# A two-layer recurrent kernel: 64x128 tiles for the first part of its one-layer score blocks, filler matmuls in the first two steps and the last, and its own order for the first and last steps

## The chip, the cores and the metric

The kernel runs on one core of a Trainium2 chip. The metric is the device time of one execution in microseconds (us). TensorE (PE in the profile) multiplies matrices into PSUM, which has eight banks here; ScalarE (ACT) and VectorE (DVE) copy results out of PSUM and do the softmax and layer norms; GpSimd (POOL) does small copies; SyncE (SP) issues nearly all transfers. An engine runs its own queue in order and waits on semaphores for the others.

## The reference, cut to what matters

```python
def _A_ref(x, mem0, Wq, Wk, Wv, Wo, seg_len):      # 64 segments of 32 rows, 16 heads of 256
    mem = mem0                                      # 8 rows
    for s in range(n_seg):
        xs = x[:, s * seg_len:(s + 1) * seg_len, :]
        h = jnp.concatenate([mem, xs], axis=1)      # 40 rows of 448
        q, k, v = (einsum('btd,dhe->bhte', h, W) for W in (Wq, Wk, Wv))
        scores = einsum('bhqe,bhke->bhqk', q, k) * scale    # masked: memory seen by all, rest causal
        p = _softmax(scores)
        o = einsum('bhte,hed->btd', einsum('bhqk,bhke->bhqe', p, v), Wo)
        mem = o[:, :M, :]                           # carried to the next segment
        outs.append(o[:, M:, :])

def _B_ref(x, W_gate, W_up, W_down):                # 448 -> 1792 -> 448
    gate, up = x @ W_gate, x @ W_up
    return (relu(gate) * up) @ W_down

x = x + _A_ref(_layernorm(x), ...);  x = x + _B_ref(_layernorm(x), ...)
x = x + _A_ref(_layernorm(x), ...);  x = x + _B_ref(_layernorm(x), ...)   # the same weights again
```

The loops above are shortened; x has 2048 rows. The memory carried from segment to segment makes each A layer a chain of 64 steps.

## The kernel before, in words

The two A layers run interleaved. Step t works on segment t of layer 0 and segment t - 4 of layer 1 (`LAG`, line 29), so there are 68 steps. Steps 0 to 3 have layer 0 alone and steps 64 to 67 layer 1 alone: the eight one-layer steps, in which the moving operand of most matmuls has 40 columns (the 40 rows of one segment) and not 80.

In `setup` (line 602) the weights come in by SP and are multiplied once: Wq with Wk into M, 56 blocks of 128 columns (`Mw`, and for the last 64 of the 448 rows `M3`), and Wv with Wo into N (`Nw`). N's products are still being made while step 0 goes on. Then a step does this:

- `t_block` (line 905) makes T = M times h, 48 + 8 blocks in three groups (`BLOCKS`, line 967). In the first two groups the rows 384 to 447 come first: `first` (line 920) multiplies them as 64x64 tiles, four matmuls for a pair of blocks, in four quarters of the array. `rest` (line 935) adds the other three 128-row parts at 128x128. `t_copies` (line 949) brings the result to `TTm` and `TTs`.
- `s_mem` (line 979) makes the scores of the 8 memory rows and their softmax, `p_t_mem` (line 1050) transposes the probabilities on TensorE, `u_mem` (line 1067) multiplies them with h, and `un_mem` (line 1080) with N in 56 matmuls of 128x32 tiles. `hi` and `lo` are its result as two bf16 parts. From these `m_t` (line 1099) and `m_nat` (line 1120) make the memory rows for the next step. This is the chain from step to step.
- `s_seg` (line 1001), `seg_pt` (line 1040) and `u_seg` (line 1152) do the same for the 32 rows of the segment; the transpose is a transfer (`tdma`, line 900), in the last step four TensorE transposes.
- After each odd step, `un` (line 1195) multiplies the segments' rows with N, `halves` (line 1188) adds the two halves of its PSUM bank and x on DVE, `ln_b` (line 878) normalizes, and `b_layer` (line 1233) does B, its last part named b_down. The last step has two of these b_layers.

`warm` (line 894) issues n matmuls of the identity with 512 columns, whose result nobody reads. It is used once, in `un` of the last pair: `S.warm(8, O.res(), [])`, after the call of `halves`. The matmuls name `un`'s bank O as read, which orders them behind `un`.

What stands where is decided when the program is built. Each operation is recorded with what it reads and writes, with a cost and a tile mode (`mm`, line 806); `_Order.run` (line 323) then lists all of them, each time taking among the operations that could start first the one with the smallest key. It picks PSUM banks, and ACT or DVE where both may copy. The key of a TensorE operation is a number by hand, `SLOT` (line 177), by name and by step modulo 4, plus a period of 86000 for each four steps; other keys are worked out from those that follow. `BIAS` (line 163) adds a number by kind of operation; TensorE operations of the steps before 4 and from 64 on have biases of their own (`@a`, `@z`; `bias_keys`, line 218). Changing these numbers changes no operation, only its place.

`_Sched._need` (line 68) then makes the semaphore waits in that order. It has one rule for PSUM that matters here:

```python
if r[0] == "ps":
    for src, val in self.readers.get(r, {}).items():
        if src != eng:
            want(src, val)
```

An operation that reads a bank also waits for those reads of another engine that stand before it in the order.

Of the kernel before, what the change touches and what calls it, by code (L numbers as in the profile page):

```python
# [44 lines left out]
class _Sched:  # L45
# [118 lines left out]
    "t_block@a": 1812, "t_blockm+": -9357, "t_blocks+": -8, "s_mem+": -142986, "p_t_mem@a": 31328, "p_t_mem+": -7192,  # L164
    "u_mem@a": 13521, "u_mem+": 747, "un_mem@a": -12628, "un_mem+": -15687, "un_memh+": -12449, "m_t@a": 6986,
    "m_t+": 6465, "m_tk+": -7932, "s_seg@a": 8100, "s_seg+": -15857, "seg_pt+": -131, "u_seg@a": 3317,
    "u_seg0+": -34358, "u_seg1+": -19122, "u_seg2+": 20412, "u_seg3+": 10778, "m_nat@a": 16787, "m_nat+": 67952,
    "t_block0f+": 11522, "t_block0r+": -14766, "t_block1r+": 16356, "ln_a+": 2229, "ln_ac+": -36153, "un@a": 57889,
    "un+": -5801, "ln_b+": -22707, "b_layer@a": -6365, "b_layer+": 479, "b_down@a": -28772, "b_down+": -16128,
    "m_natx+": 65420, "m_nat@z": -27634, "s_mem@z": 9161, "p_t_mem@z": -19432, "u_mem@z": -334, "un_mem@z": 8381,  # L170
    "m_t@z": 18252, "s_seg@z": -4933, "u_seg@z": 6743, "un@z": -14160, "b_layer@z": 39068, "b_down@z": -1631,
    "seg_pt@z": -26944, "ln_b@z": 196, "stay": 33066, "win": 142,
# [5 lines left out]
    "t_block0f.0@0": 23150, "t_block0r.0@0": 20466, "t_block0r.1@0": 10373, "t_block0r.2@0": -118963,  # L178
    "t_block0r.3@0": -102813, "t_block0r.4@0": -15176, "t_block0r.5@0": 95232, "t_block1f.0@0": 88326,
    "t_block1r.0@0": 70572, "t_block1r.1@0": -90708, "t_block1r.2@0": -669, "t_block1r.3@0": 23477,  # L180
    "t_block2r.0@0": 105637, "s_mem.0@0": -153732, "p_t_mem.0@0": -26811, "u_mem.0@0": -7044, "un_mem.0@0": 68017,
    "m_t.0@0": -385871, "s_seg.0@0": 180805, "u_seg0.0@0": 16616, "u_seg1.0@0": -3087, "u_seg2.0@0": 182854,
    "u_seg3.0@0": -7016, "m_nat.0@1": 15351, "t_block0f.0@1": -101435, "t_block0r.0@1": 175650,
    "t_block0r.1@1": -16550, "t_block0r.2@1": -78417, "t_block0r.3@1": -96693, "t_block0r.4@1": -96697,
    "t_block0r.5@1": -76748, "t_block1f.0@1": 94756, "t_block1r.0@1": -93576, "t_block1r.1@1": -61388,
    "t_block1r.2@1": 13060, "t_block1r.3@1": 192482, "t_block2r.0@1": 98249, "s_mem.0@1": 6005,
    "p_t_mem.0@1": -100695, "u_mem.0@1": 172343, "un_mem.0@1": 413220, "m_t.0@1": 76060, "s_seg.0@1": 89640,
    "u_seg0.0@1": 96587, "u_seg1.0@1": -148969, "u_seg2.0@1": 71131, "u_seg3.0@1": -99947, "un0.0@1": 269897,
    "un0.1@1": -174852, "un0.2@1": 156565, "un0.3@1": -89383, "un1.0@1": 70834, "un1.1@1": 69072, "un1.2@1": -29917,
    "un1.3@1": 26881, "un2.0@1": -89787, "un2.1@1": -86447, "un2.2@1": -10845, "un2.3@1": 13517, "un3.0@1": 89653,  # L190
    "un3.1@1": 89684, "b_layerf.0@1": 94811, "b_layer.0@1": 48867, "b_layer.1@1": 96741, "b_layerf.1@1": 109098,
    "b_layer.2@1": -3240, "b_layer.3@1": 70642, "b_down.0@1": 354372, "b_down.1@1": 72900, "b_down.2@1": 254015,
    "b_down.3@1": 240246, "b_down.4@1": 326259, "b_down.5@1": 354136, "b_down.6@1": 78849, "m_nat.0@2": 168132,
    "t_block0f.0@2": -10118, "t_block0r.0@2": -98052, "t_block0r.1@2": -41109, "t_block0r.2@2": 66134,
    "t_block0r.3@2": 13073, "t_block0r.4@2": -14618, "t_block0r.5@2": -188807, "t_block1f.0@2": -3221,
    "t_block1r.0@2": -1996, "t_block1r.1@2": -186700, "t_block1r.2@2": 70640, "t_block1r.3@2": -74211,
    "t_block2r.0@2": 16205, "s_mem.0@2": -92464, "p_t_mem.0@2": -20075, "u_mem.0@2": -252353, "un_mem.0@2": -101434,
    "m_t.0@2": 84256, "s_seg.0@2": 96377, "u_seg0.0@2": 90135, "u_seg1.0@2": 97804, "u_seg2.0@2": 182858,
    "u_seg3.0@2": 260389, "m_nat.0@3": 151329, "t_block0f.0@3": -2977, "t_block0r.0@3": -188538,
    "t_block0r.1@3": 75914, "t_block0r.2@3": -96292, "t_block0r.3@3": 6194, "t_block0r.4@3": -75085,  # L200
    "t_block0r.5@3": 69297, "t_block1f.0@3": -185930, "t_block1r.0@3": 111423, "t_block1r.1@3": -36939,
    "t_block1r.2@3": 10926, "t_block1r.3@3": 370, "t_block2r.0@3": 12228, "s_mem.0@3": -124071, "p_t_mem.0@3": 180760,
    "u_mem.0@3": 6506, "un_mem.0@3": 65274, "m_t.0@3": -389, "s_seg.0@3": -12148, "u_seg0.0@3": -75151,
    "u_seg1.0@3": 176089, "u_seg2.0@3": 78879, "u_seg3.0@3": 340369, "un0.0@3": -161383, "un0.1@3": -95386,
    "un0.2@3": 323286, "un0.3@3": 5996, "un1.0@3": 11452, "un1.1@3": 76963, "un1.2@3": -93171, "un1.3@3": -179086,
    "un2.0@3": 162572, "un2.1@3": -2533, "un2.2@3": -15402, "un2.3@3": 334269, "un3.0@3": -77062, "un3.1@3": 94056,
    "b_layerf.0@3": 350365, "b_layer.0@3": 277881, "b_layer.1@3": 268897, "b_layerf.1@3": 354905,
    "b_layer.2@3": 181729, "b_layer.3@3": 192495, "b_down.0@3": 101118, "b_down.1@3": 346959, "b_down.2@3": -2948,
    "b_down.3@3": -287771, "b_down.4@3": 93426, "b_down.5@3": 159732, "b_down.6@3": 83157, "m_nat.0@0": -484,
    "un0.4@3": -268098, "un0.5@3": -13365, "un0.6@3": 248971, "un0.7@3": -102719, "un1.4@3": 260089, "un1.5@3": -4388,  # L210
    "un1.6@3": -67736, "un1.7@3": -9258, "un2.4@3": 265064, "un2.5@3": 334268, "un2.6@3": 332162, "un2.7@3": 163179,
    "un3.2@3": 8603, "un3.3@3": -7565, "b_layer.4@3": -10753, "b_layer.5@3": 79668, "b_layer.6@3": 131945,
    "b_layer.7@3": 253283, "b_layer.4@1": 182601, "b_layer.5@1": 61111, "b_layer.6@1": 10905, "b_layer.7@1": -174890,
    "seg_pt.0@3": -162209, "un.0@3": 195399, "ln_b.0@1": 303926,
# [3 lines left out]
def bias_keys(o):  # L218
    if not o.cat:
        return []  # L220
    if o.kind != "pe":
        return [o.cat + o.sub + "+"]
    return [o.cat + "@a"] if o.t < LAG else [o.cat + "@z"] if o.t >= NSEG else []
# [19 lines left out]
class _Order:  # L243
# [13 lines left out]
    def add(self, kind, eng, cost, fn, rd, wr, name=None, mode=0, lat=None, alt=None, base=(0, 0)):  # L257
        o = _Op()
        o.kind, o.eng, o.cost, o.fn, o.rd, o.wr, o.name, o.mode = kind, eng, cost, fn, list(rd), list(wr), name, mode
        o.alt, o.base = alt, base  # L260
        o.succs, o.np, o.alloc, o.fixed, o.lat, o.cat, o.sub, o.t = [], 0, [], None, lat, self.cat, self.sub, self.t
        o.slot = None
        if kind == "pe" and o.cat:
            name = o.cat + o.sub
            i = self.count[name] = self.count.get(name, -1) + 1
            o.slot = f"{name}.{i}@{o.t % 4}"
        self.ops.append(o)
        return o
# [195 lines left out]
def MM(out, lhsT, rhs, **kw):  # L464
    return (out, lhsT, rhs, kw)


class _Kernel:
# [16 lines left out]
    def alloc(self):  # L485
# [37 lines left out]
        self.lo = self.sb("lo", [128, D])  # L523
        self.ident = self.sb("ident", [128, 128])
# [369 lines left out]
    def warm(self, n, rd, wr):  # L894

        S = self
        T = S.tile("R", 1)
        S.mm(lambda: [MM(T.b()[:, 0:512], S.ident[:, :], S.N[:, 0:2, 0:256], start=True, stop=True) for _ in range(n)], n * S.pitch(512), rd, T.res() + wr)
# [6 lines left out]
    def t_block(self, t, units):  # L905
# [14 lines left out]
        def first():  # L920
            out = []
            for a, b in zip(range(0, len(units), 2), range(1, len(units), 2)):
                for j in range(units[a][2]):
                    for o, x in ((0, a), (0, b), (1, a), (1, b)):
                        c, u0, m = units[x]
                        side, slot = S.PLACE[16 * c + u0 + j]
                        h, g = slice(64 * side, 64 * side + 64), slice(64 * o, 64 * o + 64)
# [3 lines left out]
        if pair:  # L931
            S.mm(first, sum(u[2] for u in units[::2]) * S.pitch(n) + 25.0, rd, [r for x in R for r in x.res()] + [k for u in units for k in keys(*u)], mode=3)
# [46 lines left out]
    def s_mem(self, t):  # L979
# [7 lines left out]
             [("TTm",) + k for k in S.TKEYS] + [("hTx", pp, s, l) for l in range(l0, l1)] + S.mkeys(pp, s, l0, l1), C.res())  # L987
# [13 lines left out]
    def s_seg(self, t):  # L1001
# [5 lines left out]
        def mms():  # L1007
            b = G.b()
            out = []
            for l in range(l0, l1):  # L1010
# [9 lines left out]
             [("mask", 0), ("TTsz", 0), ("TTsz", 1)] + S.mkeys(pp, s, l0, l1), G.res())  # L1020
# [19 lines left out]
    def seg_pt(self, t):  # L1040
        S = self
        if t == NSTEP - 1:

            T = S.pe_transpose([("Ps",)], lambda a: S.Ps[:, a, :], [("PTs",)])
# [5 lines left out]
    def p_t_mem(self, t):  # L1050
# [3 lines left out]
        S.mm(lambda: [MM(pT()[:, 0:128], S.Pm[:, :], S.ident[:, :], is_transpose=True)], 60.0, [("Pm",), ("ident",)], C.res() + [("PTm",)])  # L1054
# [12 lines left out]
    def u_mem(self, t):  # L1067
# [6 lines left out]
             [r for l in C for r in C[l].res()] + [("UTm", S.win(t), l) for l in C], mode=3)  # L1074
# [291 lines left out]
```

## Time and profile before

| what | value |
|---|---|
| median of three runs | 1564.83 us (1560.64 to 1566.0) |
| profiled execution, its own time | 1565.71 us |
| its span | 1563.9 us |
| PE busy | 1505.9 us, 96% of the span, 37969 matmuls |
| weight loads (PEld) busy | 1106.3 us, 71% |
| DVE and ACT busy | 868.0 us (56%) and 858.3 us (55%) |
| chain that ended last | 92% PE, 3% DVE, 2% SP's queue, 2% ACT |
| mean granted TensorE clock | 0.99 |

The profile is one execution. Its page gives busy time and granted clock in slices, and the costliest groups of instructions; the trace behind it gives each instruction's start and what it waited for. All matmuls stand under line 138, as one helper issues them, so they are told apart by tile names: b is a PSUM bank, `big` holds the B weights, the segments' U and, early, some of the attention weights. "Nw,UTm" are `un_mem`, "Nw,big" `un` (early also N's products), "hT,Mw" and "hT,M" the T blocks, "xBT,big" and "big,hB" b_layer.

### The profile page before, as it was taken

The numbers are of one execution on the slowest core, as the hardware profiler recorded it, in microseconds if no ns is written. First come the engines' busy times: TensorE is split into PE (matmuls) and PEld (weight loads), VectorE is DVE, ScalarE is ACT, GpSimd is POOL, SyncE is SP. The second block draws the span as 40 slices with busy tenths as digits, with TensorE's granted clock in tenths as the row PEclk, the third lists the DMA queues.
The fourth block names the chain that finished last, engine by engine and source line by source line (L and its number), as shares of the span: only waits on it lengthen the run. The fifth ranks groups of instructions, "written<-read, shape, count | busy, mean of one in ns | idle before, by whom it ended". The sixth has DMA issues, their size and how long they took to land.

```text
span 1563.9 us, 81992 instructions
## 1 busy us (share of the span) xinstructions
PE 1505.9 (96%) x37969; PEld 1106.3 (71%) x37969; DVE 868.0 (56%) x2353; ACT 858.3 (55%) x2599; POOL 112.0 (7%) x259
## 2 busy tenths in 40 slices
PE   5889999999999999999999999999999999999997
PEld 2457667777677777777677777777677777777665
DVE  7434565655555655555555655555564655555554
ACT  5734555655555565655555565555555555555432
POOL 4000000000000000000000000000000000000000
PEclk9989999999999999999999999999999999999998
DMA  8841001000010100000011100101010100000000
GB/s 182 205 117 35 19 18 20 18 17 16 20 20 12 25 15 20 17 15 20 16 20 15 24 15 16 19 16 21 16 21 14 22 18 15 15 18 19 15 19 14
DMA packets 129735, 46.01 MB, mean 29 GB/s; under 512 B 117736, under 2 KB 129264, under 8 KB 129392
## 3 DMA queue, kind: packets, MB, share of 16 engines
q1 hardware_dynamic: 129040, 40.53, 12.4%
q8 instruction: 298, 4.88, 1.3%
q14 instruction: 45, 0.37, 0.1%
q10 hardware_dynamic: 352, 0.24, 0.1%
HBM read 10.33 MB, written 1.84 MB: 8 GB/s over the span
## 4 chain that ended last, share of the span: by engine, by line
PE 92%; DVE 3%; SPq 2%; ACT 2%; issue 1%; DMA 1%; POOL 0%; POOLq 0%; DVEq 0%
PE b L138 92%; SPq L622 2%; ACT hi L1096 1%; ACT big L798 1%; DVE UTm L799 1%; DMA Nw<-in_A_Wo_dram 0%; DVE selm L658 0%; DMA PTs<-Ps 0%; DVE seln L661 0%; DVE stat L845 0%; DVE part L1192 0%; DVE lo L1097 0%; ACT UTm L798 0%; DVE big L799 0%; DVE xn L852 0%
## 5 line engine op out<-in xcount | busy, mean ns | idle before, releaser
L138 PE MATMUL b<-hT,Mw 128*128 128x80 bf16 (+1 forms) x11424 | 436.7, 200 | 9.2 <-issue 8.6
L138 PEld LDWEIGHTS b<-hT,Mw 128*128 128x128 bf16 x11424 | 415.3, 100 | 22.7 <-issue 14.3
L138 PE MATMUL b<-Nw,big 128*32 128x448 bf16 (+1 forms) x3540 | 295.1, 356 | 1.8 <-DVE big L799 0.8
L798 ACT ACTIVATE TTs<-b 128x320 bf16<-128x320 f32 (+5 forms) x658 | 278.4, 426 | 3.7 <-PE b L138 3.7
L798 ACT ACTIVATE TTm<-b 128x80 bf16<-128x80 f32 (+5 forms) x658 | 153.2, 235 | 137.7 <-PE b L138 131.9
L138 PEld LDWEIGHTS b<-Nw,big 128*32 128x32 bf16 (+1 forms) x3540 | 136.4, 97 | 108.8 <-issue 2.4
L138 PE MATMUL b<-xBT,big 128*128 128x128 bf16 (+3 forms) x4900 | 208.7, 215 | 0.7 <-ACT xBT L798 0.7
L138 PEld LDWEIGHTS b<-xBT,big 128*128 128x128 bf16 (+1 forms) x4900 | 187.6, 102 | 19.3 <-issue 7.1
L138 PE MATMUL b<-Nw,UTm 128*32 128x448 bf16 x3752 | 193.5, 358 | 5.3 <-DVE UTm L799 3.6
L138 PEld LDWEIGHTS b<-Nw,UTm 128*32 128x32 bf16 x3752 | 97.2, 98 | 91.2 <-DVE UTm L799 10.0
L798 ACT ACTIVATE big<-b 128x512 bf16<-128x512 f32 (+1 forms) x258 | 128.5, 560 | 35.2 <-PE b L138 35.0
L799 DVE CAST TTm<-b 64x64 bf16<-64x64 f32 (+4 forms) x226 | 48.6, 216 | 176.3 <-PE b L138 174.7
L138 PE MATMUL b<-hT,M 64*64 64x80 bf16 (+2 forms) x7208 | 142.8, 198 | 2.0 <-DVE M L799 1.2
L138 PEld LDWEIGHTS b<-hT,M 64*64 64x64 bf16 (+1 forms) x7208 | 110.9, 108 | 28.0 <-ACT hT L798 7.1
L799 POOL COPY hK<-xn 32x448 bf16<-32x448 bf16 x136 | 75.1, 552 | 657.3 <-DVE xn L852 651.0
L798 ACT ACTIVATE UTm<-b 128x512 bf16<-128x512 f32 (+1 forms) x144 | 78.3, 567 | 74.3 <-PE b L138 74.3
L1263 ACT ACTIVATE gT<-b 128x512 bf16<-128x512 f32 (+2 forms) x128 | 69.4, 542 | 62.1 <-PE b L138 50.2
L138 PE MATMUL b<-big,hB 128*128 128x448 bf16 (+1 forms) x574 | 100.1, 354 | 0.7 <-DVE hB L1264 0.7
L1264 DVE TENSOR_TENSOR hB<-gT,b 128x512 bf16<-128x512 bf16 (+2 forms) x128 | 79.3, 619 | 38.1 <-ACT gT L1263 21.8
L798 ACT ACTIVATE hT<-b 64x16 bf16<-64x16 f32 (+1 forms) x134 | 24.0, 179 | 125.9 <-DVE hT L799 88.0
L799 DVE CAST TTs<-b 64x256 bf16<-64x256 f32 (+4 forms) x226 | 90.5, 401 | 2.7 <-PE b L138 2.6
L1096 ACT ACTIVATE hi<-b 128x448 bf16<-128x448 f32 x67 | 36.5, 544 | 91.6 <-PE b L138 91.6
(112 smaller groups left out, 1625.4 us busy)
## 6 DMA issues: line engine op xcount, KB each, us to landing
big<-in_A_Wo_dram SPq DMA_DIRECT2D x3, 896.0 KB, 6.0
out_dram<-ys SPq DMA_DIRECT2D x32, 56.0 KB, 2.0
big<-in_B_W_up_dram SPq DMA_DIRECT2D x7, 224.0 KB, 2.9
big<-in_B_W_gate_dram SPq DMA_DIRECT2D x7, 224.0 KB, 3.3
big<-in_B_W_down_dram SPq DMA_DIRECT2D x7, 224.0 KB, 2.6
XA<-in_A_x_dram SPq DMA_DIRECT2D x28, 56.0 KB, 2.3
PTs<-Ps SPq DMA_TRANSPOSE x67, 2.4
Nw<-in_A_Wo_dram SPq DMA_DIRECT2D x1, 896.0 KB, 6.1
```

The costliest lines, as they stand in the source:

```text
L138: ins = E.matmul(out, lhsT=lhsT, rhs=rhs, **kw)
L622: S.q.add("dma", ("sp",), {"sp": 6200.0 if w == "Wv" and q else 4100.0}, lambda E: E.dma_start_transpose(out=st[w, q], in_=src[w][:, q * 1 ...
L798: return E.activation(out(), src(), ACT.Copy)
L799: return E.tensor_copy(out(), src())
L1096: S.act(lambda E: E.activation(S.hi[:, :], C.b()[:, 0:D], ACT.Copy), D, C.res(), [("hi",)])
L1263: S.act(lambda E, g=g, R=R, n=n: E.activation(S.gT[:, g, 0:n], R[0].b()[:, 0:n], ACT.Relu), n, R[0].res(), [("gT", g)])
L1264: S.dve(lambda E, g=g, R=R, n=n, fcs=fcs: E.tensor_tensor(S.hB[:, fcs[0]:fcs[-1] + 1, 0:w], S.gT[:, g, 0:n].rearrange("p (a b) -> p a b", ...
```

## The change

Five things:

- In one-layer steps `first` uses tiles of 64 rows by 128 columns: two matmuls for a pair of blocks in place of four. Two-layer steps keep 64x64.
- `fill` puts `warm(2)` calls, each an operation of its own with a slot, into steps 0 and 1 (two behind `s_mem`, one behind `u_mem`) and into step 67 (three behind `s_seg`). `p_t_mem`, `un_mem` and the last `seg_pt` name ("filled", t) as read, so that the fillers come before them on TensorE. `warm` multiplies M in place of N.
- The slots of steps 0 to 3 and 64 to 67 are named apart (`@a0`, `@z3`), and all slots have new numbers: 491 in place of 175. The biases of TensorE operations are gone; the others have new numbers.
- `hi` and `lo` can be one stacked part (`stacked`), which is switched off: it returns False.
- Two SBUF tiles for that, `sumA` and `sumB`, unused.

```diff
 def bias_keys(o):
     if not o.cat:
         return []
-    if o.kind != "pe":
-        return [o.cat + o.sub + "+"]
-    return [o.cat + "@a"] if o.t < LAG else [o.cat + "@z"] if o.t >= NSEG else []
+    return [] if o.kind == "pe" else [o.cat + o.sub + "+"]
...
-            o.slot = f"{name}.{i}@{o.t % 4}"
+            o.slot = f"{name}.{i}@" + (f"a{o.t}" if o.t < LAG else f"z{o.t - NSEG}" if o.t >= NSEG else str(o.t % 4))
...
-        S.mm(lambda: [MM(T.b()[:, 0:512], S.ident[:, :], S.N[:, 0:2, 0:256], start=True, stop=True) for _ in range(n)], n * S.pitch(512), rd, T.res() + wr)
+        S.mm(lambda: [MM(T.b()[:, 0:512], S.ident[:, :], S.M[:, 0, 0:4, :], start=True, stop=True) for _ in range(n)], n * S.pitch(512), rd, T.res() + wr)
+
+    def fill(self, t, n):
+        S = self
+        if t < 2 or t == NSTEP - 1:
+            cat, S.q.cat = S.q.cat, "fill" + S.q.cat
+            for _ in range(n):
+                S.warm(2, [("gap", t)], [("filled", t)])
+            S.q.cat = cat
...
-                    for o, x in ((0, a), (0, b), (1, a), (1, b)):
+                    for o, x in ((0, a), (0, b), (1, a), (1, b)) if l1 - l0 == 2 else ((-1, a), (-1, b)):
                         c, u0, m = units[x]
                         side, slot = S.PLACE[16 * c + u0 + j]
-                        h, g = slice(64 * side, 64 * side + 64), slice(64 * o, 64 * o + 64)
+                        h, g = slice(64 * side, 64 * side + 64), slice(64 * o, 64 * o + 64) if o >= 0 else slice(0, 128)
...
-             [("TTm",) + k for k in S.TKEYS] + ... + S.mkeys(pp, s, l0, l1), C.res())
+             [("TTm",) + k for k in S.TKEYS] + ... + S.mkeys(pp, s, l0, l1), C.res() + [("gap", t)])
+        S.fill(t, 2)
...
+        if t == NSTEP - 1:
+            S.fill(t, 3)
...
-            T = S.pe_transpose([("Ps",)], lambda a: S.Ps[:, a, :], [("PTs",)])
+            T = S.pe_transpose([("Ps",), ("filled", t)], lambda a: S.Ps[:, a, :], [("PTs",)])
...
-        S.mm(lambda: [MM(pT()[:, 0:128], S.Pm[:, :], S.ident[:, :], is_transpose=True)], 60.0, [("Pm",), ("ident",)], C.res() + [("PTm",)])
+        S.mm(lambda: [MM(pT()[:, 0:128], S.Pm[:, :], S.ident[:, :], is_transpose=True)], 60.0, [("Pm",), ("ident",), ("filled", t)], C.res() + [("PTm",)])
```

The order that is built from it, against the order before: TensorE has 37569 matmuls in place of 37969, SP's queue is the same but for one exchanged pair near the end. In the first steps the last N products stand behind `s_mem` of step 0, not ahead of it. In the middle the operations are the same, with some of `un`'s matmuls a few places away. At the end `un`'s last 112 matmuls stand together, 48 b_layer matmuls follow, then the eight of `warm`, and 20 b_down matmuls stand between the last transposes and the last b_layer.

## The prediction

> **What bounds the kernel now.** I read first the page's strip of 40 slices, for where TensorE is idle or slow.
>
> ```profile
> PE   5889999999999999999999999999999999999997
> ...
> PEclk9989999999999999999999999999999999999998
> ```
>
> Only the first three slices and the last are below nine tenths; the granted clock dips there too. Next the busy time by stage (length of the stretch, then busy time and instructions of PE, weight loads, DVE, ACT, POOL, then clock, DMA share, GB/s).
>
> ```profile
> 78.40:96.00 17.60, 13.22 (x377) 9.13 (x377) 7.04 (x29) 5.45 (x21) 0.18 (x1) 0.86 0.32 89
> 96.00:115.00 19.00, 15.95 (x409) 10.23 (x413) 7.02 (x29) 5.97 (x23) 0.18 (x1) 0.77 0.51 151
> ...
> 223.90:311.80 87.90, 87.30 (x2224) 65.62 (x2224) 49.79 (x131) 50.27 (x152) 5.77 (x15) 1.00 0.10 18
> ...
> 1536.00:1564.00 28.00, 22.82 (x471) 13.63 (x468) 8.69 (x16) 5.06 (x10) 0.00 (x0) 0.80 0.03 6
> ```
>
> A period of four steps in the middle takes 88 us, with PE busy for 87.3 at full clock: only its own work counts there. At the ends PE idles and the clock falls to 0.77. So I read the TensorE timeline of the first steps (start, duration, tile shape, count; in brackets the idle time before and what ended it).
>
> ```profile
> 81.87 4.06 PE L138 MATMUL b<-Nw,UTm 128*32 128x448 bf16 x56 [0.64 <-ACT UTm L798]
> 88.33 0.66 PE L138 MATMUL b<-hT,M 64*64 64x40 bf16 x60 [0.33 <-ACT hT L798]
> 88.92 2.19 PE L138 MATMUL b<-hT,Mw 128*128 128x40 bf16 x81
> 93.88 2.03 PE L138 MATMUL b<-hT,Mw 128*128 128x40 bf16 x63 [1.49 <-issue]
> 98.20 0.29 PE L138 MATMUL b<-ident,Pm 128*128 128x128 bf16 x1 [1.08 <-DVE Pm L999]
> 100.02 5.21 PE L138 MATMUL b<-Nw,UTm 128*32 128x448 bf16 x56 [0.64 <-ACT UTm L798]
> 118.23 2.82 PE L138 MATMUL b<-Nw,UTm 128*32 128x448 bf16 x56
> ```
>
> The same 56 matmuls take 2.82 us at full clock, 4.06 in step 0 and 5.21 in step 1. The trace's clock record drops to one half at 81.0 (3.4 us), 94.65 (10.2 us), 132.2 (3.4 us) and 1535.1 (10.2 us), each time behind idle time. The 1.49 us before 93.88 is a wait for nothing shown ("issue"); seven such, of 6.05 us together, lie in one-layer steps (1.49, 0.36, 0.46, 1.38, 0.70, 0.82, 0.84). Last the end, on PE and DVE:
>
> ```profile
> 1533.42 0.51 PE L138 MATMUL b<-PTs,hK 40*64 40x512 bf16 x4
> 1535.66 0.61 PE L138 MATMUL b<-ident,Ps 128*128 128x128 bf16 x4 [1.73 <-DVE Ps L1038]
> ...
> 1541.19 5.22 PE L138 MATMUL b<-Nw,big 128*32 128x448 bf16 x64
> 1546.24 0.36 PE L138 MATMUL b<-big,hB 128*32 128x448 bf16 x4
> 1546.43 2.44 PE L138 MATMUL b<-Nw,big 128*32 128x448 bf16 x48
> 1548.80 1.90 PE L138 MATMUL b<-Nw,ident 128*128 128x512 bf16 x8
> ...
> 1550.74 0.62 DVE L1192 TENSOR_TENSOR part<-b,XA 64x448 f32<-64x448 f32 x1 [8.12 <-PE b L138]
> ```
>
> 1.73 us idle, then ten at half clock (64 matmuls in 5.05 us, 48 in 2.37). And DVE starts on `un`'s result only at 1550.74, though its last matmul ended near 1548.9: in this order the eight `warm` matmuls stand in front, name that bank as read, and DVE's semaphore value is theirs.
>
> **What the skill says.** "TensorE: Matmul & The Clock Gate", Part 1: the clock falls to one half after an idle window of about 3.4 us and rises after a busy one. The trace agrees on 0.5 and on 3.4 us steps; it also drops after windows with only 1.0 to 1.7 us of idle time. Its section on Weight-path perf modes has fast weight load on when there are 128 weight columns, and "TensorEngine Tiling (Array Packing)", Restrictions, has column tiling switch it off. That fits 64x64 at 40 columns: (0.59 us less 0.09 for a switch) / 60 = 8.3 ns each, 33 ns a group of four, against 2.04 / 81 = 25 ns for a full 128x128 matmul. The same page, Key Properties: a change of mode drains the array; start to start, 64x64 to 128x128 takes 115 ns, some 90 too many.
>
> **The change, part by part**, against the profiled execution's 1565.71 us (span 1563.9), 0.9 above the median.
>
> *64-row, 128-column tiles.* In the 8 one-layer steps 100 matmuls of 64x64 become 50 of 64 rows by 128 columns: 800 become 400, in 200 pairs. The trace has no such pair. Bounds: 25.5 ns with fast load (200 x -7.5 = -1.5 us); 66 ns if a tile takes 128 columns at the 33 ns per 64 seen (+6.6). I take -1.3.
>
> *Fewer instructions.* T blocks of one layer go from 316 to 266 matmuls. The trace's instruction queue brings 16 KB, 128 matmuls with their loads, every 3.4 to 4 us at its fastest: 27 ns a matmul, 8.5 us for 316, used in about 6.7. For 266 it is 7.2 against 6.5. The shortfall falls from 1.8 to 0.7 us a step, so I take 60% of the 6.05 us away: -3.6 (ends 0 and -6).
>
> *Fillers, steps 0 and 1.* Each `warm(2)` is two 512-column matmuls; from the eight above, 1.72 / 8 = 0.215 us each. In step 1 four (0.86) stand in the 1.08 us softmax gap and two (0.43, plus switches) in the 0.64 us before `un_mem`: 0 at full clock; at half clock the four would take 1.72 and cost 0.6. In step 0 the new order puts thirteen N products behind `s_mem`, so the gaps of 0.30, 1.08 and 0.32 are filled with due work (-1.70) and four fillers are pure cost (+0.86): -0.84. Behind them on ACT stand eleven copies of 0.49 us and PTm, UTm; banks are what could run late.
>
> *Clock.* With step 0 busy, `un_mem` takes 2.82: -1.24. Step 1's drop cost 2.39 in `un_mem` and some 0.7 around; it followed the 1.49 us stall; half taken, -1.5. Step 3's (140 matmuls in 4.56 us, 56 x 8.8 + 84 x 29.3 ns, start to start at full clock, = 2.96) followed the 1.38 us stall; half, -0.8.
>
> *End.* Six fillers (1.29), four u_seg and 24 b_layer matmuls now stand between `s_seg` and the transposes: the 1.73 us gap is closed, -0.44. The half clock then has no cause. What stood in it: `un` 2.2 us too long, b_layer 0.98 + 0.69, u_seg 0.7, transposes 0.3: -4.8. In the new order 48 b_layer matmuls precede the eight `warm`; DVE waits for `un` alone: -1.76, less 0.4, as 20 b_down matmuls now stand before the last b_layer: -1.4.
>
> *Mode switches.* 796 become 783: -1.2.
>
> *Tables.* In the middle the new order has the same matmuls in the same tiles with the same switches, 2224 a period; `un` matmuls move by a few places beside m_t and T blocks, and remain at least 1.9 us where the uncovered hi/lo wait at 163.5 was 1.30. ACT and DVE exchange one or two copies of a period, at 50 of 88 us busy; POOL takes one copy earlier; SP's order is unchanged but for one pair at the end. 0, with 15 periods x 0.2 = 3 us either way.
>
> Sum: 1.3 + 3.6 + 0.84 + 1.24 + 1.5 + 0.8 + 0.44 + 4.8 + 1.4 + 1.2 = 17.1 us. I give back 2.5 for waits that the new order makes itself (bank waits in step 0, m_nat among the T blocks of step 66): 1565.7 - 14.6 = **1551 us**, 0.9% under the median.
>
> **Rivals.**
> *The clock still falls at the end.* The windows run free of the program, and a 40-row u_seg or a stall may count as idle. For: it fell at 132.2 after 0.9 us of idle time in the window. Against: with the gap closed only two issue stalls are left between 1523 and the end of `un`. 4.8 and about 1 more stay: 1557.
> *The head doesn't gain.* Issue stalls come with the place of a refill and not with the rate, and step 1's clock with them: 3.6 + 1.5 + 0.8 + 1.24 stay: 1558. With both, 1564: no change. For: a 1.06 us stall at 1314 in a two-layer step. Against: seven of them in eight short steps.
> *Slower: the new tiles load slowly.* The clock page's LDWEIGHTS section prices a load at columns / 1.2 ns, 107 ns for 128; if both of a pair are paid in turn, 200 x (214 - 33) = +36 us, 1589. It decides above about 33 + 13300 / 200 = 100 ns a pair. Against: 64x64 loads of 64 columns overlap fourfold (33 ns for four), and full 128-column loads keep a 25 ns pace.
>
> **Chances and range.** Forecast 0.60 (own range 1546 to 1555); clock falls at the end 0.15; no gain in the head 0.08; both 0.07; slow loads or a middle slower by over 1 us a period 0.07; better than forecast 0.03. Faster by over 0.3% (under 1560.1; a run of this kernel can't tell less, its three lie 5.4 us apart): 0.83; within 0.3%: 0.10; slower: 0.07. 1545 to 1561 holds 8 in 10.
>
> **What would show it.** 64x128 pairs near 25 ns; `un_mem` of steps 0 and 1 at 2.8 us; issue stalls of the one-layer steps under 3 us in all; no clock drop from 1530 to 1550; DVE's last part<-b,XA within 0.3 us of `un`'s end; middle periods of 88.3 us in the mean, as before. Wrong if they exceed 88.6, if pairs take over 40 ns, or if step 0's `un_mem` waits for Nw copies beyond 82.

## The result, and the profile after

The kernel after takes 1539.99 us (median of four runs, 1539.38 to 1542.49), the kernel before beside it 1562.74: the ratio is 0.9858, with a 95% interval of 0.983 to 0.9887. That is 22.7 us less, where 13.8 less than the median shown were forecast, and the time lies under the lower end of the range, 1545. The sign was right, and the mechanism in the main; the size was too small. Measured again later, the kernel after took 1542.99 us, ratio 0.9876 (0.9853 to 0.9899), 19.8 less.

The profiled execution after took 1539.38 us, with a span of 1537.6. The strip of its page, in 40 slices:

```profile
PE   5999999999999999999999999999999999999998
...
PEclk9999999999999999999999999999999999999999
```

Only the first slice and the last are now below nine tenths. The clock reads nine tenths or more in every slice, and the record behind the strip is full from 36.3 us to 1538.2. This is one execution, with a mean clock of 0.999; the other runs of this kernel here and below read 0.997 to 0.999, so by estimate most of them have one or two stretches of 3.4 us at half clock more, at places not known. The busy time by stage, with the columns as before (length, then busy time and instructions of PE, weight loads, DVE, ACT, POOL, then clock, DMA share and GB/s); the stretches are step 1's and step 2's chain, one period of four steps, and the last 28 us:

```profile
75.00:89.60 14.60, 13.44 (x340) 8.95 (x337) 7.04 (x26) 7.02 (x23) 0.18 (x1) 1.00 0.38 106
89.60:105.70 16.10, 14.85 (x376) 9.93 (x381) 7.28 (x34) 5.79 (x21) 0.18 (x1) 1.00 0.57 159
212.97:300.77 87.80, 86.89 (x2220) 65.54 (x2224) 49.80 (x130) 49.31 (x150) 5.28 (x14) 1.00 0.08 18
1509.60:1537.60 28.00, 23.99 (x640) 16.13 (x637) 12.88 (x31) 10.24 (x32) 0.00 (x0) 1.00 0.08 14
```

The clock reads 1.00 where before it read 0.86, 0.77 and 0.80, and the last 28 us hold 640 matmuls where they held 471. The TensorE timeline of the first steps (start, duration, tile shape, count, idle time before and what ended it):

```profile
78.53 2.83 PE L138 MATMUL b<-Nw,UTm 128*32 128x448 bf16 x56
...
90.55 0.81 PE L138 MATMUL b<-Mw,ident 128*128 128x512 bf16 x3
91.57 0.23 PE L138 MATMUL b<-ident,Pm 128*128 128x128 bf16 x1 [0.21 <-DVE Pm L1077]
...
93.14 2.83 PE L138 MATMUL b<-Nw,UTm 128*32 128x448 bf16 x56
...
99.20 0.54 PE L138 MATMUL b<-hT,M 64*128 64x40 bf16 x30
99.67 1.70 PE L138 MATMUL b<-hT,Mw 128*128 128x40 bf16 x60
```

`un_mem` takes 2.83 us in both steps (4.06 and 5.21 before). The fillers ("Mw,ident", four in the program; a few matmuls have no record) leave 0.21 us of the 1.08 us before the transpose of Pm. The 30 matmuls of 64x128 take 0.47 us from start to start, less 0.09 for a switch of tile mode: 12.7 ns each, 25.3 ns a pair. Waits for nothing shown ("issue") were 8.6 us in the whole kernel, 6.05 of them in one-layer steps. The waits after (total, times, longest):

```profile
PE b L138 <- issue: 3.8, 8, 0.9
```

In one-layer steps two are left, 0.84 and 0.33 us: 1.17. The end, on PE and DVE:

```profile
1514.13 1.24 PE L138 MATMUL b<-Mw,ident 128*128 128x512 bf16 x5
...
1516.14 0.40 PE L138 MATMUL b<-ident,Ps 128*128 128x128 bf16 x4
...
1518.65 5.48 PE L138 MATMUL b<-Nw,big 128*32 128x448 bf16 x112
...
1524.18 0.62 DVE L1289 TENSOR_TENSOR part<-b,XA 64x448 f32<-64x448 f32 x1 [5.31 <-PE b L138]
```

`un`'s last 112 matmuls take 5.48 us in one piece, where 64 and 48 of them took 5.05 and 2.37, and DVE starts at once (the next matmuls of another kind began at 1524.06).

Where the 26.3 us between the two spans lie, from the start of `un_mem` in each step (last `un` matmul for step 67):

| stretch | before | after | difference |
|---|---|---|---|
| to `un_mem` of step 0 | 81.87 | 78.53 | -3.34 |
| steps 1, 2, 3 | 57.39 | 48.53 | -3.55 -2.23 -3.09 |
| steps 4, 5 | 40.17 | 41.60 | +0.57 +0.86 |
| steps 6 to 63 | 1276.71 | 1272.86 | -3.8 |
| steps 64, 65, 66 | 62.95 | 60.08 | -0.29 -1.06 -1.53 |
| step 67 to the end of `un` | 29.43 | 22.18 | -7.24 |
| from there to the last matmul | 11.35 | 9.77 | -1.58 |

### The profile page after: what moved, and what is told of

It is laid out like the page before. It is cut to its first block, busy times and chain, and to the rows that moved or that the text cites. A ratio compares the mean times of both kernels' runs of the same rounds, so it can differ in the third digit from the quotient of the medians.

```text
span 1537.6 us, 81239 instructions
## 1 busy us (share of the span) xinstructions
PE 1492.6 (97%) x37565; PEld 1099.6 (72%) x37569; DVE 882.2 (57%) x2381; ACT 849.2 (55%) x2571; POOL 112.5 (7%) x259
## 4 chain that ended last, share of the span: by engine, by line
PE 92%; DVE 3%; SPq 2%; ACT 2%; issue 1%; DMA 0%; POOL 0%; POOLq 0%
PE b L138 92%; SPq L690 2%; ACT hi L1183 1%; DVE UTm L867 1%; ACT big L866 1%; DMA Nw<-in_A_Wo_dram 0%; DVE selm L726 0%; DVE seln L729 0%; DVE stat L913 0%; DVE lo L1184 0%; DVE part L1289 0%; DVE big L867 0%; DVE xn L920 0%; DVE stat L1113 0%; DVE Es L1114 0%
## 5 line engine op out<-in xcount | busy, mean ns | idle before, releaser
L866 ACT ACTIVATE TTs<-b 128x320 bf16<-128x320 f32 (+5 forms) x650 | 273.8, 424 | 0.8 <-PE b L138 0.7
L138 PE MATMUL b<-Nw,UTm 128*32 128x448 bf16 x3752 | 189.7, 353 | 4.6 <-DVE UTm L867 4.4
L138 PE MATMUL b<-hT,M 64*64 64x80 bf16 (+3 forms) x6808 | 142.8, 199 | 1.0 <-issue 0.5
L138 PEld LDWEIGHTS b<-hT,M 64*64 64x64 bf16 (+2 forms) x6808 | 109.5, 107 | 30.5 <-ACT hT L866 10.8
L866 ACT ACTIVATE UTm<-b 128x448 bf16<-128x448 f32 (+2 forms) x132 | 72.4, 563 | 68.5 <-PE b L138 68.4
L867 DVE CAST TTs<-b 64x256 bf16<-64x256 f32 (+4 forms) x234 | 95.3, 407 | 1.2 <-PE b L138 1.2
L867 DVE CAST UTm<-b 128x448 bf16<-128x448 f32 (+2 forms) x119 | 69.0, 589 | 38.5 <-PE b L138 37.9
```

The source lines that it names most:

```text
L138: ins = E.matmul(out, lhsT=lhsT, rhs=rhs, **kw)
L866: return E.activation(out(), src(), ACT.Copy)
L867: return E.tensor_copy(out(), src())
```

## The experiments

The ratios are to the kernel before, run beside each; "less" is worked out from the ratio, of 1563 us. Below, a stall is a wait of TensorE for nothing shown, and a drop is a stretch in which the clock record of the profiled execution reads one half.

### The parts alone, from the kernel before

Theory A: TensorE runs short of instructions in one-layer steps, the clock falls behind that, and fewer matmuls cure both. Rival B: the new tables and the fillers did it by filling the gaps. First the 64x128 tiles alone; the order stays the same on every engine. (With the tiles the mode number that the planner is told goes from 3 to 1, here and wherever these tiles change below.)

```diff
-                    for o, x in ((0, a), (0, b), (1, a), (1, b)):
+                    for o, x in ((0, a), (0, b), (1, a), (1, b)) if l1 - l0 == 2 else ((-1, a), (-1, b)):
...
-                        h, g = ..., slice(64 * o, 64 * o + 64)
+                        h, g = ..., slice(64 * o, 64 * o + 64) if o >= 0 else slice(0, 128)
```

> The kernel before with the 64x128 pairs alone; its order stays the same on every engine. Theory A (TensorE's instructions don't come in fast enough in the one-layer steps, and half clock follows those stalls): the issue stalls of the one-layer steps fall from 6 us to under 2.5, the clock drops that followed a stall (near 94 and 132 us) go, the drop near 81 and the one at the end stay; 5 to 9 us faster. Theory B (the new order did nearly all): 200 pairs at 25 in place of 33 ns, 1.3 to 2.5 us faster, with the stalls and the drops where they were.

Measured: 1556.21 us, ratio 0.9953 (0.9938 to 0.9968), 7.3 us less. Issue stalls of one-layer steps fall from 6.05 to 0.33 us. The clock drop of step 3 is gone with its stall; those of the head are not, and the one at the end stays, at 1529.81. The TensorE timeline of the head:

```profile
78.95 0.23 PE L138 MATMUL b<-ident,Pm 128*128 128x128 bf16 x1 [1.08 <-DVE Pm L999]
80.72 5.40 PE L138 MATMUL b<-Nw,UTm 128*32 128x448 bf16 x56 [0.64 <-ACT UTm L798]
```

No stall stands between step 0 and step 1 any more, and still the clock record drops at 79.15, 89.39 and 99.63. The softmax gaps do that by themselves. A holds for the stalls and the time, and fails for the head's clock.

Then the new tables alone: the kernel after with 64x64 tiles and no filler.

```diff
-        if t < 2 or t == NSTEP - 1:
+        if False:
...
-                    for o, x in ((0, a), (0, b), (1, a), (1, b)) if l1 - l0 == 2 else ((-1, a), (-1, b)):
+                    for o, x in ((0, a), (0, b), (1, a), (1, b)):
```

> The kernel after without fillers and with 64x64 tiles, so the new slots and biases alone. Theory A: the issue stalls of 4 to 6 us in the one-layer steps come back and with them one to three clock drops, the end's among them as its 1.7 us gap is open again; 8 to 13 us faster than before. Theory B: 17 to 22 us faster.

Measured: 1556.39 us, 0.9962 (0.9947 to 0.9977), 5.9 less, under both theories. Stalls of one-layer steps add to 4.61 us, and the clock drops at 84.42, 94.66 and 179.99. It doesn't drop at the end, and step 67 is 6.2 us shorter. That holds for this profile and is in part luck: gaps of 1.45 and 0.69 us stand before the last b_layer, the same that half clock follows in two runs below, and here the border of a 3.41 us window of the clock record (last section) lies between them.

Next both code changes under the tables of before (shown against the kernel after; the numbers of the tables go back too).

```diff
-    return [] if o.kind == "pe" else [o.cat + o.sub + "+"]
+    if o.kind != "pe":
+        return [o.cat + o.sub + "+"]
+    return [o.cat + "@a"] if o.t < LAG else [o.cat + "@z"] if o.t >= NSEG else []
...
-            o.slot = f"{name}.{i}@" + (f"a{o.t}" if o.t < LAG else f"z{o.t - NSEG}" if o.t >= NSEG else str(o.t % 4))
+            o.slot = f"{name}.{i}@{o.t % 4}"
```

> Pairs and fillers with the slots and biases of the kernel before. Theory A: stalls under 2.5 us, at most one clock drop; 10 to 16 us faster than before. Theory B: 3 to 6 us faster.

Measured: 1552.99 us, 0.9937 (0.9913 to 0.9961), 9.8 less, about what A said. Stalls of one-layer steps are 2.69 us. No drop in the head, but one of 6.8 us at 1539.55, beside a gap of 2.29: in the old tables the end fillers have no place of their own.

Last the fillers alone: before's tables, 64x64 tiles, `fill` called as in the kernel after.

> The kernel before with the fillers alone: its own tables (the fillers have no slots in them), 64x64 tiles. With it all eight combinations of pairs, tables and fillers have a time but for chip-to-chip difference: none 1563, pairs 1556, tables 1556, both 1548.5, pairs and fillers 1553, tables and fillers 1552, all 1540 to 1543. Theory S (the parts only pay together, since an idle piece that stays in a window keeps the half clock): the fillers alone gain little, as step 1's stall of 1.49 us and the tail's 1.7 us stay: 1560 to 1563. Rival T (the parts add up: fillers are worth the 3 to 4 us that they add to one other part): 1558.5 to 1560.

Measured: 1559.91 us, 0.9978 (0.9968 to 0.9988), 3.4 less: theory T. Stalls stay at 5.83 us. The clock now holds in the steps 0 and 1 and drops in step 2, at 108.49 (behind a stall of 1.32), and at the end, at 1548.91 (behind a gap of 2.29).

One step of the forecast was tried by itself. Here `warm` no longer names bank O, so that DVE can't wait for it:

```diff
-                S.warm(8, O.res(), [])
+                S.warm(8, [("XB", (p + 1) % 2, 1)], [])
```

> The kernel before, its eight filler matmuls after the last un ordered behind DVE's read of un's bank, so that DVE no longer waits for them. Both theories: DVE's last part<-b,XA begins within 0.3 us of un's end, and the time falls by 1.4 to 1.8 us. If the wait was hidden, 0.

Measured: 1563.76 us, 0.9999 (0.9986 to 1.0011). In the trace DVE now begins at `un`'s end (1546.89, with the last `un` matmuls starting before 1546.7), and the stretch from there to the last matmul is 10.24 us in place of 11.35. That is 1.1 us in the trace, where 1.4 to 1.8 were expected; the medians don't show it.

### The parts taken away, from the kernel after

64x64 tiles back:

```diff
-... if l1 - l0 == 2 else ((-1, a), (-1, b)):
+...:
```

> The kernel after with 64x64 tiles back in the one-layer steps; fillers and tables stay. Theory A2 (the pairs end the issue stalls because they halve the matmuls; the early fillers hold the clock; the tables close the end): 4 to 7 us of issue stalls in the one-layer steps again and perhaps one clock drop behind one of them; 6 to 9 us slower than the kernel after, so 1546 to 1549. Theory B2 (with gaps filled the stalls hide): 1 to 3 us slower, 1541 to 1543.

Measured: 1552.33 us, 0.993 (0.9905 to 0.9956), 12.3 and 9.3 us more than the two medians of the kernel after. The clock holds (no drop from 29.3 to 1551.6), but eight stalls of 0.66 to 1.02 us, 6.88 in all, are back in the one-layer steps. Its waits on nothing shown, in the whole kernel:

```profile
PE b L138 <- issue: 9.6, 15, 1.0
```

So the new order doesn't cure them, and filled gaps hide none: A2, but for the clock, which needs no pairs to hold. Tiles and order are not quite apart here: with the mode number the planner chose another order near the end, from 1474 us on. In the steps 0 to 3 the order is the same, and there stalls are 3.51 us as against 0.84. Of the 12.4 us between this span and that of the kernel after, 5.7 are stalls of one-layer steps, 1.5 the slower groups of four, 0.8 a later Wo block and 2.9 lie between the steps 8 and 60, where the two kernels are alike; 1.5 have no account.

No filler at all (`if False:` in `fill`):

> The kernel after without any filler; pairs and tables stay. A2: the clock drops once or twice between 80 and 105 us again, not at the end; 1 to 4 us slower than the kernel after. B2 (each set of fillers holds the clock where it stands): it drops at the end too, 6 to 9 us slower.

Measured: 1548.52 us, 0.9904 (0.9888 to 0.9919). The clock drops at 91.59 for 6.8 us, at 1521.77 and at 1538.84. The end of its TensorE timeline:

```profile
1537.27 0.40 PE L138 MATMUL b<-ident,xn 128*128 128x128 bf16 x4 [1.45 <-DVE xn L920]
1538.35 4.70 PE L138 MATMUL b<-xBT,big 64*64 64x64 bf16 x140 [0.69 <-ACT xBT L866]
```

The same 140 matmuls take 3.20 us after. B2 holds: the end needs its fillers. Without fillers before the transposes the planner runs half of the 48 b_layer matmuls ahead of `un`, so that less is left to cover DVE after it. DVE itself is later too: from its start on `un`'s result to the end of `xn` it takes 5.4 us, as against 3.4 in the kernel after, as other work stands ahead and it waits for the `warm` matmuls again:

```profile
1534.41 0.63 DVE L1290 TENSOR_TENSOR XB<-b,part 64x448 bf16<-64x448 f32 x1 [0.51 <-PE b L138]
```

Behind the 1.45 us the clock falls. So the fillers work through the order too, not only by keeping TensorE busy.

Early fillers alone (`if t < 2:`):

> The kernel after with the fillers of steps 0 and 1 alone, none in step 67. A2: no clock drop at the end, 1 us faster to 0.5 us slower than the kernel after, as six fillers of 1.3 us are gone and the gap is filled by real work. B2: a drop of 3 to 10 us at the end, 2 to 5 us slower.

Measured: 1548.11 us, 0.9903 (0.9888 to 0.9918). A2 falls: the end isn't closed by tables and pairs. The drops at 1519.95 and 1537.02 are there, as without any. The head, whose order is that of the kernel after, has one too, at 86.35.

End fillers alone (`if t == NSTEP - 1:`):

> The changed kernel with the fillers of the last step alone, none in steps 0 and 1. With the earlier runs this makes a square of four: without any 1548.5, early ones alone 1548.1, both 1540. Theory P (each set of fillers holds the clock where it stands): the record drops to one half once near 92 us, as without any filler, for 6.8 us, which makes step 2 longer by about 2.6 us in the trace, and the end is as in the changed kernel: 1541 to 1544. Rival Q (early fillers cost on full-speed steps what they save, as the two runs with and without them, 0.4 us apart, say): 1539 to 1541.

Measured: 1541.42 us, 0.9864 (0.9842 to 0.9886), beside 1542.99 for the kernel after. The figure lies in P's range and 0.4 us above Q's; beside it the kernel after took 1.6 us more, so by time the early fillers are worth nothing that shows, as Q has it. P has the trace: the clock drops at 93.00, for 3.4 us and not 6.8. In the traces the early fillers cost about what the forecast said (`un_mem` of step 0 begins 23.16 us after the wait for the Wo block with them and 22.39 without any, +0.77) and save 1.5 and 1.8 us in steps 1 and 2, as that drop is gone.

### Whether the number of matmuls makes the stalls

Each 64x128 matmul of 40 columns is cut into two of 20, so that a T block takes 316 matmuls from the queue again, in the good tiles:

```diff
-... else ((-1, a), (-1, b)):
+... else ((-1, a), (-1, b), (-2, a), (-2, b)):
...
-                        out.append(MM(R[x].b()[g, j * n:j * n + n], S.M3[h, slot, g], mov(3, h), start=(j == 0), stop=False))
+                        q, v = (0, mov(3, h)) if o >= 0 else (20 * (-1 - o), S.hT[h, pp, 3, l0:l1, s, 20 * (-1 - o):20 * (-1 - o) + 20])
+                        w = n if o >= 0 else 20
+                        out.append(MM(R[x].b()[g, j * n + q:j * n + q + w], S.M3[h, slot, g], v, start=(j == 0 and o != -2), stop=False))
```

> The changed kernel, in which each 64x128 matmul of 40 columns of the one-layer T blocks is cut into two of 20: the same tiles and the same result, but four matmuls a group again, 316 a T block instead of 266, as with 64x64 tiles. Theory C (TensorE runs short of instructions: what counts is how many matmuls a step takes from the queue): the issue stalls of the one-layer steps come back, to 5 to 7 us in all as with 64x64 tiles in this order (9.6 us in the whole kernel instead of 3.8), and the time is near that kernel's 1552: 1547 to 1553. Rival F (the form counts: 64x64 tiles at 8 ns apiece and the switch of mode drain the queue or the array, and wide tiles don't): stalls stay near 3.8 us in all, and only the cuts' own time is added, at most 200 pairs x 15 ns = 3 us: 1540 to 1543.

Measured: 1551.46 us, 0.9927 (0.9899 to 0.9954): within theory C's range, but not for C's reason alone. Its timeline and its waits:

```profile
102.37 0.91 PE L138 MATMUL b<-hT,M 64*128 64x20 bf16 x60
103.22 1.70 PE L138 MATMUL b<-hT,Mw 128*128 128x40 bf16 x60
```

```profile
PE b L138 <- issue: 6.7, 11, 1.0
```

A 20-column matmul takes (0.85 - 0.09) / 60 = 12.7 ns, as much as one of 40 columns, so the cuts cost 200 x 25.3 = 5 us themselves, not at most 3. The stalls of one-layer steps come back to 3.85 us in seven pieces (1.17 and 1.73 in the two profiles after), short of the 5 to 7 expected; that slower groups also use the supply more slowly may be why. That stalls grow with the number of matmuls is shown in tiles that didn't change. The kernel after beside it took 1542.99 us; of the 8.5 us between them the cuts are 5 and the stalls 2.1. The rest holds a clock drop at 86.46, behind the two gaps of 0.44 and 0.45 us that the kernel after has there too.

What a stall waits for can be read from the traces. Instructions come in over a transfer queue of their own, in blocks of 16 KB. In the kernel before it brought 298 (packets, MB, share of 16 engines), one for each 127 of the 37969 matmuls with their weight loads:

```profile
q8 instruction: 298, 4.88, 1.3%
```

From 70 us on, the sixteen profiles of this study have 150 stalls of 0.15 us or more. 148 of them ended 1.20 to 1.61 us after a block had landed; of the 906 other waits of TensorE 11% did. So a stall is a wait for the next block of instructions.

### What goes further

64x128 tiles in two-layer steps too, 3000 matmuls fewer:

```diff
-... if l1 - l0 == 2 else ((-1, a), (-1, b)):
+                    for o, x in ((-1, a), (-1, b)):
...
-... mode=3 if l1 - l0 == 2 else 1)
+... mode=1)
```

> The kernel after with the pairs of 64x128 tiles in the two-layer steps as well, 3000 matmuls fewer. At 80 columns a group of four 64x64 takes 36 ns and a pair can't take less than the full array's 36, so the T blocks gain nothing; A2: the few issue stalls of the middle (1 to 3 us in all) go, 0 to 3 us faster. B2: no difference, within 1 us.

Measured: 1535.2 us (1533.38 to 1536.88), 0.9819 (0.9804 to 0.9835): ahead of both kernels, 4.8 us under the kernel after, whose second median lies higher still. That is more than either theory said. The order is the same on TensorE, DVE and ACT. Its stalls are 1.8 us in the whole kernel, as against 3.8:

```profile
PE b L138 <- issue: 1.8, 3, 0.8
```

And the T blocks do gain. The first group of a two-layer step, in the kernel after and here:

```profile
305.86 0.73 PE L138 MATMUL b<-hT,M 64*64 64x80 bf16 x60
306.52 2.43 PE L138 MATMUL b<-hT,Mw 128*128 128x80 bf16 x63
...
304.15 0.71 PE L138 MATMUL b<-hT,M 64*128 64x80 bf16 x30
304.79 2.43 PE L138 MATMUL b<-hT,Mw 128*128 128x80 bf16 x63
```

From start to start it is 0.66 us and 0.64; the second group gains 0.02 us too, and 60 steps x 0.04 make 2.4 us.

Then the first products of b_layer as 64x128 as well (28 matmuls for 56 in each of 35 b_layers, 980 fewer; the 420 of the expectation counts one b_layer for each four steps):

```diff
-                return [MM(R[x].b()[64 * o:64 * o + 64, i * w:i * w + w], S.W3[64 * x:64 * x + 64, fc * 128 + 64 * o:fc * 128 + 64 * o + 64],
+                return [MM(R[x].b()[:, i * w:i * w + w], S.W3[64 * x:64 * x + 64, fc * 128:fc * 128 + 128],
                            S.xBT[64 * x:64 * x + 64, 3, r], start=(i == 0), stop=False)
-                        for _, fcs, R in units for i, fc in enumerate(fcs) for o in range(2) for x in range(2)]
+                        for _, fcs, R in units for i, fc in enumerate(fcs) for x in range(2)]
...
-            S.mm(first, sum(sizes) * S.pitch(w) + 10.0, rd, res + hk, mode=3)
+            S.mm(first, sum(sizes) * S.pitch(w) + 10.0, rd, res + hk, mode=1)
```

> The kernel with 64x128 pairs in all T blocks (1535.2), and in b_layer's first products too: 28 matmuls of 64 rows by 128 columns for 56 of 64x64 (14 and 12 in the one-layer steps' b_layer in the same way). Theory C (number of matmuls and switches): 28 x 15 = 420 matmuls and some 40 switches of mode fewer[...]: 0 to -2 us, 1533 to 1536. Rival F: no difference, 1535 to 1536.

Measured: 1764.58 us, 1.1293 (1.126 to 1.1326), 229 us more than without. Both theories missed that. Its waits:

```profile
PE b L138 <- DVE Pm L1077: 39.3, 28, 2.2
PE b L138 <- DVE lo L1184: 35.3, 33, 1.8
PE b L138 <- ACT hT L866: 19.3, 14, 1.5
```

In the kernel without it, those on Pm don't show among the eleven longest and lo and hT are 2.9 and 0.5. The planner takes what can start first and adds a switch where the mode number differs; with another number for these products it chose another order, from 282 us on in the trace, and slots tuned for the old one no longer cover the softmax. The clock falls behind these waits: its mean is 0.956 in this run. To tell order from tiles, the same tiles with the number kept:

```diff
-            S.mm(first, sum(sizes) * S.pitch(w) + 10.0, rd, res + hk, mode=1)
+            S.mm(first, sum(sizes) * S.pitch(w) + 10.0, rd, res + hk, mode=3)
```

> As the kernel with 64x128 pairs in all T blocks and in b_layer, but the planner is told for b_layer's first products the mode number that they had, so that the order stays: only the tiles differ. Theory O (the 1764.6 us came from the order that the planner made once those products had another mode number: its waits on Pm, lo, hT and TTm grew by over 100 us): 1533 to 1537. Rival W (64x128 tiles with the W3 weights or 128 moving columns are slow themselves): over 1600.

Measured: 1537.63 us, 0.9834 (0.9817 to 0.9851): theory O, 0.6 us above its range. The 229 us came from the order. Stalls fall to 0.4 us in the whole kernel, but it isn't ahead of 1535.2; its profile has a drop at 84.83.

The kernel after once more:

> The changed kernel again, unchanged, so that the three others of this call stand beside it on the same chip: 1539 to 1543 by both theories. Its Wo1 block lands at 55.3 to 57 us as in the other profiles, and issue stalls of the two-layer steps come at other places than in the first profile; those of the one-layer steps stay under 2 us.

Measured: the 1542.99 us given above. As expected one-layer stalls stay under 2 us: 1.73 (0.84, 0.29, 0.60). Against the expectation, three of the two-layer stalls stand where they stood in the first profile, near 244, 421 and 680 us. The clock record is full from 36.9 to 1542.1.

### All eight combinations

| with | ratio, interval | us less, of 1563 |
|---|---|---|
| pairs | 0.9953 (0.9938 to 0.9968) | 7.3 |
| tables | 0.9962 (0.9947 to 0.9977) | 5.9 |
| fillers | 0.9978 (0.9968 to 0.9988) | 3.4 |
| pairs, tables | 0.9904 (0.9888 to 0.9919) | 15.0 |
| pairs, fillers | 0.9937 (0.9913 to 0.9961) | 9.8 |
| tables, fillers | 0.993 (0.9905 to 0.9956) | 10.9 |
| all | 0.9858 (0.983 to 0.9887), 0.9876 (0.9853 to 0.9899) | 22.2, 19.4 |

The parts alone add to 16.7 us, together they give 19 to 22. The difference is of the size of the intervals, so the medians don't show that the parts help one another. The traces give a reason why they may: in the head, pairs alone leave softmax gaps of 1.69 us in one window of the clock record and fillers alone a stall of 1.32 us in another, half clock follows each, and pairs with fillers have no drop there. But tables with fillers hold the clock throughout too, with stalls of up to 1.02 us left.

## Why the prediction was wrong

The working was a list of gains, most of which came as it said, and four discounts, most of which weren't due. By its own terms, from the two profiles after:

| term of the sum | forecast | measured |
|---|---|---|
| 64-row, 128-column tiles | -1.3 | -1.5 (25.3 ns a pair for 33) |
| issue stalls of one-layer steps | -3.6, 60% of 6.05 | -4.9 and -4.3 |
| fillers and order, step 0 | -0.84 | -1.7 in both |
| clock, step 0's `un_mem` | -1.24 | -1.23 |
| clock, steps 1 and 3 | -1.5 and -0.8, half of each | the whole in these profiles, as no drop is left |
| end gap and half clock; with them the stalls of step 67 | -0.44 -4.8; -1.0 that is counted in the stalls above | -7.24 and -7.36, stalls included |
| DVE's wait on `warm` | -1.4 | -1.58 and -1.59 |
| mode switches | -1.2 | not measured apart |
| waits that the new order makes | +2.5 | steps 4 and 5: +1.43, of which 1.07 are stalls, and -0.04 |
| middle | 0 | -3.8 and -0.9 |

**Tiles, step 0, end: right.** The rival of slow loads fell at 25.3 ns a pair. "TensorEngine Tiling (Array Packing)" of the Trainium skill, Restrictions, has column tiling switch fast weight load off, and a 64x128 tile has none; its 12.7 ns agree with that, though no run here shows the weight load by itself. In step 0 `un_mem` began 3.34 us earlier; 1.64 of that is the Wo block, waited for until 57.01 before and 55.37 after, and the runs show it anywhere from 55.3 to 57.0. The 1.7 left is twice the net that the sum had: fillers cost 0.77, and the N products behind `s_mem` gave 2.5, not 1.7. The stretch up to the last `un` matmul was off by 1.0 to 1.1 us, 0.7 of them the stalls of step 67, which went whole and not by 60%. The end gained the 1.4 us of DVE's wait, and 0.2 more, though that change alone, in the kernel before, doesn't show in the medians.

**The failing step was the set of discounts.** The sum took 60% of the stalls, half of the clock loss in steps 1 and 3, and then gave back 2.5 us for waits that the new order makes itself: 7.25 us in all. Of these, 1.2 and 1.7 us of stalls did stay. The order made one wait of note (0.74 us on UTm in step 4), worth some 0.4 us in the steps 4 and 5 of the first profile and nothing in the second. So some 5.5 us were held back for nothing in these profiles (in other executions a drop or two of the clock may have been due), and 14.6 us were forecast where the medians show 22.7 and 19.8, that is 8.1 and 5.2 more. Step 0 (0.9 us), the end (1.0) and the middle make the rest. Without the four discounts the same working reads 17.1 + 2.45 + 1.5 + 0.8 = 21.85 us, between the two measured, or 1543.9 from the execution that it was taken from. The doubts that they stood for had their place already: the rivals "the head doesn't gain" and "the clock still falls at the end" held 0.30 of the chance. The likeliest case should have been worked out as if it came true, and the range carried down to the far ends named in the text (stalls "0 and -6"), where 1545 took in only part of them. "Better than forecast 0.03" was the number most in error.

**One cause was put wrong.** The forecast let step 1's half clock follow its 1.49 us stall. The kernel with pairs alone has no such stall and drops in the head all the same. So does the one with `warm`'s wait changed, whose head is that of the kernel before: no stall stands in its step 1, and the clock drops at 81.84, 88.66 and 98.90. So does the kernel after without fillers, at 91.59. In the profiles, step 3's drop is gone with each of the three parts alone. The steps 0 and 1 hold with fillers, but for a drop near 85 us in three runs of the new order (last section). The end holds in seven of seven profiles with the tables and the end fillers, with pairs and without (the order of 1764.58 us left aside).

**Rate more than place.** The rival that the head doesn't gain, as stalls come with the place of a refill and not with the rate, fell: with 64x64 tiles they add to 6.05, 4.61, 5.83 and 6.88 us in four different orders, with pairs to 0.33, 2.69, 0.70 and 1.17. Each is a wait for a block of instructions, so the order still decides where one falls, and the count how much they add to.

**The middle and the base.** The steps 6 to 63 gained 3.8 us in one profile and 0.9 in the other, where 0 was forecast. The shortest period of four steps fell from 87.96 to 87.77 us, which makes some 2.7 us in all. The rest is spread from run to run: the same stretch took 1274.9 to 1277.8 us in five profiles with the old tables and 1272.9 to 1278.6 in eight with the new ones. The profiled execution of before was 3.0 us above the median that this kernel had beside the result, and that of after 0.6 below its own, which makes the 26.3 us between the traces 22.7 between the medians.

## What to carry to other kernels

Work out the likeliest case at full size and let the doubts into the chances and the range; a discount on each term counts the same doubt twice. Look for a rival cause before a loss is put down to the gap next to it: step 1's half clock stayed when its stall was gone. Short runs of small matmuls can be bound by the supply of instructions: there, a wider tile that does the work of two pays by the count, beyond the time of the tiles (4.3 to 4.9 us of stalls here, and 1.5 of tiles). In a planned order a changed label can cost more than any tile (229 us here): keep the order fixed when a tile is to be measured.

## What the runs showed of the hardware

The clock record of each profile lies on a grid of 3.41 us whose start differs from run to run. In all sixteen profiles of this study, from 70 us on, half clock followed each of the 44 full-clock windows of this grid with 1.65 us or more without a matmul, 18 of the 145 with 0.77 to 1.61 us, and none of the 6689 with less. "TensorE: Matmul & The Clock Gate" of the Trainium skill, Part 1, speaks of an idle window; here less than half of one suffices. The same order can keep the clock or lose it with the place of the grid: the gaps of 0.44 and 0.45 us in step 0 went by in both profiles of the kernel after. In one window as well, 3.4 us of half clock followed them with early fillers alone, with the matmuls cut in two and with the mode number kept, at 86.35, 86.46 and 84.83 us, where the order of the head is the same.

Start to start, a 64x128 matmul takes 12.7 ns whether it moves 20 or 40 columns, and 17.6 at 80; a 64x64 one takes 8.1 ns at 40 columns and 9.1 at 80. Cutting the 40 columns in two bought nothing.
